# Second MoE of a three-layer kernel: row lists fetched by GpSimd through an index per partition, the late table in nine pieces, one-block row buffers and a third output buffer

## The chip, the cores and the metric

One core of one Trainium2 chip. The metric is the device time of one execution in microseconds. The kernel before takes 966.37 us (median of 3 runs, 966.15 to 967.48).

## The reference

Three layers follow one another: attention over 4 batches, 8 heads, 576 positions and 64 dimensions, with a threshold under the row maximum; a squared-ReLU feed-forward layer (512 to 2048 to 512) over the 2304 tokens, the first MoE; and a second MoE in which each token goes to one of eight experts:

```python
logits = x @ w_gate                       # 2304 x 8
e_idx = np.argmax(logits, axis=1)
...
gate_w = probs[np.arange(N), e_idx]
eom = 1.0 / (1.0 + np.exp(-(x @ w_output_gate)))
for e in range(E):
    mask = e_idx == e
    h = np.maximum(x[mask] @ w1[e], 0.0)  # w1[e]: 512 x 1024
    ye = h @ w2[e]                        # w2[e]: 1024 x 512
    out[mask] = gate_w[mask, None] * eom[mask, e, None] * ye
```

## The kernel before

**Planner.** The program is written as a graph of tasks (`Graph.add`), each with an engine, an estimated duration, what it reads and writes, and a due time, its `key`. `Graph.schedule` goes through them greedily: on each engine, of the tasks that could start within a small slack of the earliest, the one with the smallest key. Buffers come from pools (`mk` for on-chip memory, `mkps` for the product banks); a pool's slot may lie over another's that has to be done before. What comes out is one fixed order per engine. Each engine then works through its own queue in that order and stands where the head of the queue waits.

**First MoE's last tiles and the gate.** The 2304 tokens are 18 blocks of 128, two to a tile. For a tile v, `t_y` forms the layer's output from seven products (L1011) whose sums VectorE adds (L1021, L1027) into `row`; `t_gate` transposes the two blocks (L1161 on TensorE, L1166 ScalarE, L1167 VectorE), multiplies them by the gate's weights (L1076, transposed back at L1085), picks the expert (L1095 to L1107), ranks tokens by products with triangular matrices (L1113), computes each token's place in its expert's list (L1127 to L1133) and the gate's factor (L1138 to L1141). The rows with their factor go to DRAM (`y_scr`, L1151, SyncE's queue), and GpSimd scatters pairs (row, token) to their places in a DRAM list `lst` (L1147). The last tile, v = 8 (blocks 16 and 17), is called y8 below.

**Slots.** The second MoE runs in slots, each one expert's rows: "p" has 256 rows (two blocks), "s" 128, "W" 288 (two blocks and a remainder of 32). Two early slots, e0 and e1, use lists that an early table draws up when some tiles are done; they run while the first MoE ends. A late table (`t_table(False)`, L1206 to L1256 on VectorE, one task) sets up the rest: `tab2` for p, `tab1` for s, `tabw` for W, each with a list start and an expert number. The ten late slots follow the string `ORDER`. A branch on `tabn` (L1533, L1534), taken only if more slots are needed, stands within the last one.

`t_slot` does, for each slot: SyncE reads the list's start (`r_s`) and the expert (`r_e`) into registers; SyncE loads the slot's piece of `lst` (`f_list`, L1285; L1287 for a remainder); GpSimd gathers the rows of `y_scr` block by block into one three-block buffer `xg` (L1295); SyncE loads eight halves of a megabyte of weights into staging buffers `raw` (L1309 for w1, L1312 for w2; four buffers and a fifth); ScalarE and VectorE turn each into a rounded value and a remainder (L1316, L1319) in a pool `w`; the rows are transposed like those of the gate (L1161, L1166, L1167), and ScalarE copies each row's factor into `cs` (L1325, L1330). The first product (L1342, in 96 matmuls of 256 columns for a p slot; s has its own, L1363 with transposes L1375 behind ScalarE's L1369) leaves relu on ScalarE (L1350) and the remainder on VectorE (L1353). The second product is L1429 (48 of 512 columns) for p and s, evicted by L1438 into one of two buffers `ob` and scattered to the output by GpSimd (L1441); for W it is L1395, transposed back (L1409), evicted by L1414 and scattered by L1418. The output scatters wait for one another, since all write the one output.

## Time and profile before

| | before |
|---|---|
| time, median of 3 runs | 966.37 us (966.15 to 967.48) |
| profiled execution: time, span | 964.99 us, 963.2 us |
| mean granted TensorE clock | 0.987 |
| busy: TensorE, VectorE, ScalarE, GpSimd | 926.0, 706.8, 634.3, 360.7 us |
| span from e0's first product (687.90 us) to the end | 275.3 us |

The profile is of one execution. A row of its timeline gives the start, the duration, the engine and line, and in brackets how long the engine stood idle before it and what released it. Matmuls overlap, so a row of several lasts a little longer than their pitch. The granted clock is 1.00 at TensorE's upper level. Everything before 687 us is the attention and the first MoE and is the same program in both kernels but for the order of a few tasks.

### The profile page before, as it was taken

Reading aid. Unit: us, or ns where it says so; the run is one execution under the profiler, and the core shown is the slowest. Engines: PE = TensorE matmul, PEld = TensorE weight load, DVE = VectorE, ACT = ScalarE, POOL = GpSimd, SP = SyncE. Lnnn points to the kernel's source line nnn. Section 1 sums busy time; section 2 is a strip of 40 time slices with the busy share of each in tenths; the row PEclk is TensorE's granted clock in tenths of the full one; section 3 lists DMA queues with packets and bytes.
Section 4 is the critical chain, followed back from the end, with each engine's and each line's share of the span. In section 5 each row is a group of like instructions: output and inputs, shape, how many; then the busy total and the mean of one; then the engine's idle time right before and its main releaser. Section 6 shows DMA issues by size and latency. Waiting matters only on the chain.

```text
span 963.2 us, 20472 instructions
## 1 busy us (share of the span) xinstructions
PE 926.0 (96%) x6818; PEld 843.4 (88%) x6818; DVE 706.8 (73%) x1634; ACT 634.3 (66%) x1416; POOL 360.7 (37%) x607
## 2 busy tenths in 40 slices
PE   8889999999999999999999999999898999999995
PEld 7666889889899889889999999999887989889894
DVE  6888898877777777788558776898796685774720
ACT  5788888887787777686654544445546675775821
POOL 4556778766657767652100000010112221121200
PEclk9999999999999999999999999999898999999999
DMA  6785787767787767467456898648848895795700
GB/s 177 180 198 153 207 232 205 219 163 213 222 235 224 226 199 233 146 206 238 159 148 132 184 187 182 133 127 197 264 118 302 272 309 163 250 327 191 254 33 26
DMA packets 160534, 188.68 MB, mean 196 GB/s; under 512 B 23167, under 2 KB 112767, under 8 KB 160418
## 3 DMA queue, kind: packets, MB, share of 16 engines
q1 hardware_dynamic: 156370, 177.13, 65.4%
q0 software_dynamic: 3904, 10.13, 3.1%
q8 instruction: 57, 0.93, 0.4%
q14 instruction: 59, 0.48, 0.2%
q10 hardware_dynamic: 144, 0.00, 0.0%
HBM read 117.80 MB, written 42.80 MB: 167 GB/s over the span
## 4 chain that ended last, share of the span: by engine, by line
PE 69%; DMA 10%; DVE 7%; issue 6%; ACT 4%; POOL 2%; SPq 0%; POOLq 0%; DVEq 0%; ACTq 0%
PE banks L850 18%; PE banks L1011 17%; PE banks L1342 7%; PE banks L740 6%; PE banks L643 6%; PE banks L712 6%; PE banks L1429 5%; DMA memf<-y_scr,memf 3%; PE banks L1395 2%; DMA memf<-in_moe_w_dram 2%; ACT pt L720 1%; DMA out_dram<-memf 1%; PE banks L1161 1%; DVE memf L658 1%; PE banks L1363 1%
## 5 line engine op out<-in xcount | busy, mean ns | idle before, releaser
L658 DVE SCALAR_TENSOR_TENSOR memf<-banks,memf 128x576 f32<-128x576 f32 x144 | 116.3, 814 | 44.3 <-ACT memf L649 28.3
L850 PE MATMUL banks<-memr,w 128*128 128x288 f32 x960 | 145.0, 299 | 1.4 <-DVE memr L747 1.4
L850 PEld LDWEIGHTS banks<-memr,w 128*128 128x128 f32 x960 | 130.9, 188 | 5.4 <-issue 3.8
L1011 PE MATMUL banks<-w,memr 128*128 128x256 f32 x864 | 127.2, 285 | 0.0
L720 ACT ACTIVATE pt<-banks 128x384 f32<-128x384 f32 (+2 forms) x320 | 114.4, 419 | 14.7 <-PE banks L712 13.9
L646 DVE TENSOR_REDUCE memf<-banks 128x1 f32<-128x576 f32 x144 | 107.6, 750 | 18.0 <-PE banks L643 16.4
L649 ACT ACTIVATE memf<-banks,memf 128x576 f32<-128x576 f32 x144 | 107.1, 753 | 19.9 <-DVE memf L646 14.5
L991 ACT ACTIVATE memr<-memf 128x512 fp32r<-128x512 f32 x126 | 77.5, 630 | 61.5 <-PE banks L1011 51.4
L669 POOL TENSOR_SCALAR memf<-memf 128x576 f32<-128x576 f32 x136 | 112.5, 829 | 12.7 <-DVE memf L666 6.8
L643 PE MATMUL banks<-memr 128*128 128x288 f32 x592 | 110.0, 311 | 4.8 <-DVE memf L658 3.0
L712 PE MATMUL banks<-ident,memf 128*128 128x128 f32 x720 | 106.9, 278 | 5.9 <-ACT pt L720 5.1
L1011 PEld LDWEIGHTS banks<-w,memr 128*128 128x128 f32 x864 | 112.3, 190 | 0.3
L1011 PE MATMUL banks<-memr 128*128 128x256 f32 x648 | 98.7, 283 | 0.0
L712 PEld LDWEIGHTS banks<-ident,memf 128*128 128x128 f32 x720 | 85.6, 142 | 14.6 <-POOL memf L654 4.9
L887 POOL TENSOR_TENSOR memf<-memf 128x288 f32<-128x288 f32 x88 | 72.2, 829 | 65.5 <-DVE memf L887 41.9
L643 PEld LDWEIGHTS banks<-memr 128*128 128x128 f32 x592 | 84.7, 190 | 12.8 <-DVE memf L658 6.8
L1147 POOL DMA_INDIRECT lst<-memf x18 | 18.5, 1026 | 193.5 <-DVE memf L1139 115.9
L1319 DVE TENSOR_TENSOR w<-memf,w 128x512 fp32r<-128x512 f32 x110 | 72.6, 688 | 24.5 <-ACT w L1316 20.6
L995 DVE TENSOR_TENSOR memr<-memf,memr 128x512 fp32r<-128x512 f32 x126 | 83.0, 697 | 9.5 <-ACT memr L991 9.2
L850 PE MATMUL banks<-memr 128*128 128x288 f32 x576 | 87.9, 299 | 0.8 <-ACT memf L856 0.8
L1011 PEld LDWEIGHTS banks<-memr 128*128 128x128 f32 x648 | 86.7, 191 | 0.1
L740 PE MATMUL banks<-pt,memf 128*64 128x256 f32 (+1 forms) x640 | 85.1, 411 | 1.3 <-DVE memf L658 1.0
(181 smaller groups left out, 1761.2 us busy)
## 6 DMA issues: line engine op xcount, KB each, us to landing
memf<-in_moe_w_dram SPq DMA_DIRECT2D x96, 512.0 KB
r_scr<-memf SPq DMA_DIRECT2D x192, 144.0 KB
memf<-r_scr SPq DMA_DIRECT2D x51, 512.0 KB
memr<-memr SPq DMA_DIRECT2D x64, 144.0 KB
memr<-memr SPq DMA_DIRECT2D x64, 128.0 KB
memr<-memr SPq DMA_DIRECT2D x32, 256.0 KB
memf<-in_moe_w_in_dram SPq DMA_DIRECT2D x32, 256.0 KB
memf<-in_moe_w_out_dram SPq DMA_DIRECT2D x32, 256.0 KB
```

What stands on the lines that cost most here:

```text
L643: nc.tensor.matmul(s.t[:, hf, :HALF], qo, ko[:, halves[hf]], start=(i == 0), stop=(i == len(ops) - 1))
L646: nc.vector.tensor_reduce(nm.t, s.t[:, :, :HALF], axis=AX.XY, op=ALU.max, negate=True)
L649: nc.scalar.activation(p.t[:, :S].rearrange("p (a n) -> p a n", a=2), s.t[:, :, :HALF], AF.Exp, bias=nm.t)
L658: nc.vector.scalar_tensor_tensor(p3, s.t[:, :, :HALF], th.t, p3, op0=ALU.is_ge, op1=ALU.mult, accum_out=sm.t)
L669: nc.gpsimd.tensor_scalar(p.t[:, :S], p.t[:, :S], sm.t, 1.0, op0=ALU.mult, op1=ALU.mult)
L712: nc.tensor.transpose(ps.t[:, i - a], p.t[:, i * P : (i + 1) * P], ident)
L720: lambda pt=pt, ps=ps, j=j, a=a, z=z, c0=c0, w=w, off=off: nc.scalar.activation(pt.t[:, j, a:z, off : off + w], ps.t[:, :, c0 : c0 + w], A ...
L740: nc.tensor.matmul(out(slice(64 * j, 64 * j + 64)), raw.t[:, j, c], pt.t[:, j, c, :N], start=(c == 0), stop=(c == NQ - 1))
L850: nc.tensor.matmul(ps.t[:, :HALF], wv[:, a, kc], xT.t[:, x, kc, half], start=(i == 0), stop=(i == len(seq) - 1),)
L991: g.add("ACT", c_act(512), lambda d=d, sq=sq: nc.scalar.activation(d(0), sq(), AF.Copy), [(b, j)], [(o, 0, j)], at, after=turn["op"])
L995: lambda d=d, sq=sq: nc.vector.tensor_tensor(d(1), sq(), d(0).bitcast(F32), op=ALU.subtract),
L1011: nc.tensor.matmul(ps.t[:, :QT], o.t[:, a, f], w.t[:, x, cc], start=(f == 0 and i == 0), stop=(f == 7 and i == 2))
```

## The change

- Lists. `r_s` and `f_list` are gone from SyncE. GpSimd gathers each list by an index per partition: the constants `st2`, `st1` now hold the partition's number, so that a table's entry is the row of `lst` that this partition wants. For a slot of two blocks one indirect transfer fetches two pairs per partition; an s slot has one, a W slot three, through a new table `tabv`. These are 16 transfers more on GpSimd in the slots that run, and edges (`turn["lt"]`, `turn["xg"]`) keep lists and gathers in the slots' order.
- Late table. Its operations are collected and run in nine pieces, tasks of their own, with `tab2` done after the fourth piece (`tabl` stands for the rest); the early table stays in one piece.
- Buffers. Row buffers `xg`: three of one block in place of one of three. `ob`: three in place of two. `lt`, `cs`: four in place of three. `cs` is copied block by block. With the new sizes the fifth `raw` lies over other buffers of the first MoE (parts of p1, u2, u3, u4 and lgs instead of row1, gs, p1, u2 and u3).
- Due times. The last tile's sums and gate are due `HASTE` = 10 earlier; the early slots' transposes 3 earlier, and e1's come after the last gate's transposes (an `after` edge). `ORDER` is "psWspspsWp" instead of "psWspsWspp".

```diff
-    ORDER = "psWspsWspp"
+    HASTE = 10
+    ORDER = "psWspspsWp"
...
-    at = mk("lt", at, 3, [P, 3, 2], I32, 2)
-    at = mk("cs", at, 3, [P, 3], F32, 2)
+    at = mk("lt", at, 4, [P, 3, 2], I32, 2)
+    at = mk("cs", at, 4, [P, 3], F32, 2)
...
-    mk("xg", at, 1, [P, 3, DM + 1], F32, 3)
+    mk("xg", at, 3, [P, 1, DM + 1], F32, 3)
...
-    at = mk("ob", 0, 2, [P, DM], F32, 3)
+    at = mk("ob", 0, 3, [P, DM], F32, 3)
...
+        soon = lambda i: at(i) - (HASTE if v == TILES // 2 - 1 else 0)
...
-                out(4, 1, 0, "u3", at(i + 1))
+                out(4, 1, 0, "u3", soon(i + 1))
...
+        x = grp("PE", 0.45, tp, rd, [ps], key, hold=[x2], after=after)
...
+        for u in range(2):
+            ts(tabv[:, :, u], tabw[:, :, 0], 128.0 * (u + 1), None, op0=ALU.add)
...
-        grp("DVE", (3.1 if early else 8.4), run, [(c2, "base"), (c2, "tab")], [tb, "tabe" if early else "tabl"], key)
+            second(tt, ts, stt, copy, cnt, d, a, od, tmp, Q, wn, inc, cum, slots)
+
+        def piece(lo, hi):
+            if not prog:
+                run()
+                assert len(prog) == cuts[-1], (early, len(prog))
+            for x in prog[lo:hi]:
+                x()
+
+        cuts = [0, 19] if early else [0, 8, 15, 21, 27, 33, 39, 44, 50, 55]
+        for lo, hi in zip(cuts, cuts[1:]):
+            w = ["tabe" if early else "tab2" if hi <= 27 else "tabl"]
+            k = key if hi <= 27 else key + 10
+            grp("DVE", 0.195 * (hi - lo), lambda lo=lo, hi=hi: piece(lo, hi), [(c2, "base"), (c2, "tab")], [tb] + w, k)
...
-        td = "tabe" if tab is tabe else "tabl"
-        add("SP", 0.9, r_s, [td], [("reg", tag, 0)], key - 24)
-        dma(f_list, 2048, [("reg", tag, 0)] + deps, [lt], key - 24)
+        td = "tabe" if tab is tabe else "tab2" if tab is tab2 else "tabl"
+        if U == 2 and not R:
+            lists = [(range(2), lambda: lt.t[:, :2].rearrange("p u t -> p (u t)"), lst.rearrange("(r u) t -> r (u t)", u=2), tab[:, s, 0:1])]
+        else:
+            lists = [((u,), lambda u=u: lt.t[: rows(u), u], lst, (tabv[: rows(u), s, u - 1 : u] if u else tab[:, s, 0:1]))
+                     for u in range(UR)]
+        for us, dst, src, idx in lists:
+            add("POOL", 1.05,
+                lambda dst=dst, src=src, idx=idx: nc.gpsimd.indirect_dma_start(
+                    out=dst(), out_offset=None, in_=src, in_offset=bass.IndirectOffsetOnAxis(idx.bitcast(U32), 0)),
+                [td] + deps, [(lt, u) for u in us], key - 24, lat=3.0,
+                after=turn["lt"] if G is g else ())
...
-                [lt, "y0"] + [("ys", u) for u in range((rows_known - 1) // P)], [(xg, u)], key - 12, lat=6.5)
+                [(lt, u), "y0"] + [("ys", x) for x in range((rows_known - 1) // P)], [xg[u]], key - 12, lat=9.5,
+                after=turn["xg"] if G is g else ())
...
-            t_transpose(xg, u, x2, f"x{tag}", key - 8, [(xg, u)], G, pool, rows(u))
+            t_transpose(xg[u], u, x2, f"x{tag}", key - (11 if tab is tabe else 8), [xg[u]], G, pool, rows(u),
+                        turn["gate"] if tab is tabe and s == KE - 1 else ())
```

Three places in the orders. The first is VectorE near 690 us, where y8's last sums (L1021; L1026 in the changed kernel) stand among e0's weight remainders (L1319; L1355), each row's tile `w_..` or `memr` being a weight buffer; L1167 (L1173) is the remainder of transposed rows. Before:

```order
L1319 TENSOR_TENSOR w_71<-memf,w_71 128x512
L1319 TENSOR_TENSOR memr<-memf,memr 128x512
L1021 TENSOR_TENSOR memf<-banks,memf 128x256
L1319 TENSOR_TENSOR w_75<-memf,w_75 128x512
L1319 TENSOR_TENSOR w_78<-memf,w_78 128x512
L1167 TENSOR_TENSOR memr<-banks,memr 128x4x128
L1319 TENSOR_TENSOR memr<-memf,memr 128x512 x2
L1021 TENSOR_TENSOR memf<-banks,memf 128x256
```

After:

```order
L1173 TENSOR_TENSOR memr<-banks,memr 128x4x128
L1032 TENSOR_TENSOR memf<-banks,memf 128x256
L1026 TENSOR_TENSOR memf<-banks,memf 128x256
L1355 TENSOR_TENSOR w_71<-memf,w_71 128x512
L1355 TENSOR_TENSOR memr<-memf,memr 128x512
L1026 TENSOR_TENSOR memf<-banks,memf 128x256
L1355 TENSOR_TENSOR w_75<-memf,w_75 128x512
```

The last sum now stands behind the remainders of `w_71`, ahead of two pairs that it stood behind.

The second is VectorE at the late table: the end of the last tile's place (L1133) and the table's first rows in the kernel before, and a stretch of the table (all its rows bear the line L1204) in the changed one, with L1353 (L1387), e0's relu remainder, and L1319 (L1355). Before:

```order
L1132 TENSOR_REDUCE memf<-memf 128x2
L1133 CAST memf<-memf 128x2
L1353 SCALAR_TENSOR_TENSOR memr<-banks,memr 128x256
L1206 TENSOR_TENSOR memf<-memf 128x8
L1207 COPY memf<-memf 128x8
```

After:

```order
L1204 TENSOR_TENSOR memf<-memf 128x64
L1204 TENSOR_REDUCE memf<-memf 128x8
L1204 TENSOR_TENSOR memf<-memf 128x8
L1204 CAST tabn<-memf 128x1
L1204 TENSOR_TENSOR memf<-memf 128x8
L1204 SCALAR_TENSOR_TENSOR memf<-memf 128x8
L1355 TENSOR_TENSOR memr<-memf,memr 128x512
L1204 TENSOR_TENSOR memf<-memf 128x96 x3
L1204 TENSOR_TENSOR memf<-memf 128x192
L1204 TENSOR_REDUCE memf<-memf 128x24
L1204 TENSOR_TENSOR tab_91<-memf 128x24
L1387 SCALAR_TENSOR_TENSOR memr<-banks,memr 128x256
```

The table's rows ran on to L1256 without another line between; now relu and weight remainders stand between the pieces. `tab_91` is `tab2`.

The third is GpSimd's queue from e1's gathers to p0's: list scatters L1147 (L1153), row gathers L1295 (L1328), list gathers (L1319, new), output scatters L1441 (L1475). Before:

```order
L1147 DMA lst<-memf 21760x2 x4
L1295 DMA memf<-y_scr,memf 128x513 x2
L1147 DMA lst<-memf 21760x2 x2
L1441 DMA out_dram<-memf 2304x512 x2
L1295 DMA memf<-y_scr,memf 128x513 x2
L1441 DMA out_dram<-memf 2304x512
L1295 DMA memf<-y_scr,memf 128x513
L1441 DMA out_dram<-memf 2304x512
```

After:

```order
L1328 DMA memf<-y_scr,memf 128x513
L1153 DMA lst<-memf 21760x2 x4
L1328 DMA memf<-y_scr,memf 128x513
L1153 DMA lst<-memf 21760x2 x2
L1319 DMA memf<-lst,tab_91 128x4
L1475 DMA out_dram<-memf 2304x512
L1328 DMA memf<-y_scr,memf 128x513 x2
L1475 DMA out_dram<-memf 2304x512
L1319 DMA memf<-lst,tab_92 128x2
L1319 DMA memf<-lst,tabw 128x2
```

The list gather of p0 (`tab_91`) stands right behind the last list scatters; of the two output scatters of e0 that stood before p0's row gathers, one now stands before them and one behind.

## Rows read from the trace of the kernel before

**Rows 1.** The page, part 1: busy time of each engine.

```profile
PE 926.0 (96%) x6818; PEld 843.4 (88%) x6818; DVE 706.8 (73%) x1634; ACT 634.3 (66%) x1416; POOL 360.7 (37%) x607
```

**Rows 2.** Windows by stage: start:end, length, busy time per engine (instructions), granted clock, DMA.

```profile
687.90:720.04 32.14, 28.68 (x171) 25.33 (x170) 27.23 (x104) 15.64 (x35) 1.98 (x2) 0.89 0.53 171
720.04:751.49 31.45, 26.92 (x154) 23.40 (x152) 22.75 (x41) 19.84 (x40) 8.60 (x6) 0.89 0.85 297
751.49:829.50 78.01, 76.66 (x491) 69.33 (x490) 53.08 (x91) 55.58 (x113) 14.31 (x13) 1.00 0.74 246
```

**Rows 3.** Waits of TensorE, 640 to 964 us: total, times, longest.

```profile
PE banks L1161 <- DMA memf<-y_scr,memf: 4.3, 3, 3.7
PE banks L1161 <- DVE memf L1021: 2.8, 1, 2.8
PE banks L1375 <- ACT memf L1369: 2.6, 2, 1.3
PE banks L1429 <- PEq L1534: 1.8, 1, 1.8
```

**Rows 4.** Timeline of TensorE: start, duration, operation, [idle before <-releaser].

```profile
693.14 1.11 PE L1161 MATMUL banks<-ident,memf 128*128 128x128 f32 x4 [2.78 <-DVE memf L1021]
...
694.48 0.41 PE L1342 MATMUL banks<-memr 128*128 128x256 f32 x1
...
700.15 0.28 PE L1342 MATMUL banks<-memr,w 128*128 128x256 f32 x1
...
721.56 5.01 PE L1342 MATMUL banks<-memr,w 128*128 128x256 f32 x40 [0.41 <-DVE memr L1167]
...
740.20 1.12 PE L1161 MATMUL banks<-ident,memf 128*128 128x128 f32 x4 [3.74 <-DMA memf<-y_scr,memf]
...
742.48 2.91 PE L1429 MATMUL banks<-memr 128*128 128x512 f32 x6
...
762.69 1.55 PE L1429 MATMUL banks<-memr 128*128 128x512 f32 x6
```

**Rows 5.** Timeline of VectorE, 700 to 724 us.

```profile
701.90 0.19 DVE L1095 COPY memf<-banks 128x32 f32<-128x32 f32 x1
...
706.73 0.17 DVE L1133 CAST memf<-memf 128x2 uint32<-128x2 f32 x1
...
707.14 0.16 DVE L1206 TENSOR_TENSOR memf<-memf 128x8 f32<-128x8 f32 x1
...
712.28 0.18 DVE L1203 TENSOR_TENSOR tab<-memf 128x24 int32<-128x24 f32 x1
...
717.07 0.16 DVE L1256 SCALAR_TENSOR_TENSOR tabn<-tabn,memf 128x1 int32<-128x1 int32 x1
...
721.42 2.49 DVE L1319 TENSOR_TENSOR w<-memf,w 128x512 fp32r<-128x512 f32 x4
```

**Rows 6.** Timeline of ScalarE.

```profile
690.79 1.15 ACT L1316 ACTIVATE memr<-memf 128x512 fp32r<-128x512 f32 x2 [0.32 <-DMA memf<-in_moe_w_dram]
...
822.27 0.68 ACT L1414 ACTIVATE memf<-banks,memf 32x512 f32<-32x512 f32 x1 [1.72 <-DMA out_dram<-memf]
```

**Rows 7.** Timeline of SyncE's queue, 715 to 722 us.

```profile
715.84 3.08 SPq L1312 DMA_DIRECT2D memf<-in_moe_w_dram  x2
...
721.57 0.38 SPq L1285 DMA_DIRECT2D memf<-lst  x1
```

**Rows 8.** Timeline of GpSimd, 712 to 734 us, and landings of `y_scr` transfers.

```profile
712.92 0.98 POOL L1147 DMA_INDIRECT lst<-memf  x1 [4.75 <-DMA lst<-memf]
721.71 3.08 POOL L1441 DMA_INDIRECT out_dram<-memf  x1 [7.81 <-ACT memf L1438]
731.03 0.99 POOL L1441 DMA_INDIRECT out_dram<-memf  x1 [6.24 <-DMA memf<-in_moe_w_dram]
732.32 0.98 POOL L1295 DMA_INDIRECT memf<-y_scr,memf  x1 [0.30 <-PE banks L1342]
...
DMA to landing us min/median/max: 3.6/5.8/8.1
```

More of the change, by code (lines that the diff above doesn't have):

```diff
@@ L249, in tables @@
     ctab[:, lo : lo + n] = np.arange(128)[:, None] < np.arange(128)[None, :]
+    for nm in ("st2", "st1"):
+        lo, n = CTAB[nm]
+        ctab[:, lo : lo + n : 2] += np.arange(128)[:, None]
     p = np.arange(512)
@@ L502, in moa @@
     tabw = const.tile([P, NLW, 2], I32, name="tabw")
+    tabv = const.tile([P, NLW, 2], I32, name="tabv")
     tabn = const.tile([P, 4], I32, name="tabn")
@@ L916, in moa @@
         at += n
-    assert at <= 528, at
+    assert at <= 536, at
     def cv(nm, shape=None, dt=F32):
@@ L963, in moa @@
     rows = {}
-    turn = {"op": [], "slot": 0}
+    turn = {"op": [], "slot": 0, "xg": [], "lt": []}
     def t_y(v, key):
@@ L1055, in t_gate @@
         for i in range(2):
-            t_transpose(row, i, x2, f"y{v}", key + i - 1, [(row, i, 0), (row, i, 1)])
+            turn["gate"] = [t_transpose(row, i, x2, f"y{v}", key + i - 1, [(row, i, 0), (row, i, 1)])]
         lt = Buf(ALL["lgt"], f"lgt{v}")
@@ L1168, in t_transpose, with second, later @@
             [ps, (x2, 0, i)], [(x2, 1, i)], key)
+        return x
     tb = Buf(ALL["tb"], "tb")
-    def t_table(early, key):
-        tt, ts, stt = nc.vector.tensor_tensor, nc.vector.tensor_scalar, nc.vector.scalar_tensor_tensor
+    def second(tt, ts, stt, copy, cnt, d, a, od, tmp, Q, wn, inc, cum, slots):
+        tt(cnt, d, a, op=ALU.add)
+        cum(od)
+        copy(tabn[:, 1:2], inc[:, 7:8])
+        stt(Q[:, 0], cnt, 256.0, ct("ebd"), op0=ALU.mult, op1=ALU.add)
+        slots(NL1, tab1, False)
+        cum(wn)
+        copy(tabn[:, 2:3], inc[:, 7:8])
+        stt(Q[:, 0], od, 128.0, Q[:, 0], op0=ALU.mult, op1=ALU.add)
+        slots(NLW, tabw, False)
+        for u in range(2):
+            ts(tabv[:, :, u], tabw[:, :, 0], 128.0 * (u + 1), None, op0=ALU.add)
+        ts(tmp[:, 0:1], tabn[:, 0:1], float(S2), None, op0=ALU.subtract)
+        stt(tmp[:, 0:1], tabn[:, 1:2], float(S1), tmp[:, 0:1], op0=ALU.subtract, op1=ALU.max)
+        stt(tabn[:, 3:4], tabn[:, 2:3], float(SW), tmp[:, 0:1], op0=ALU.subtract, op1=ALU.max)
+    def t_table(early, key):
+        prog = []
+        def later(fn):
+            return lambda *a, **k: prog.append(lambda: fn(*a, **k))
+        tt, ts, stt = (later(x) for x in (nc.vector.tensor_tensor, nc.vector.tensor_scalar, nc.vector.scalar_tensor_tensor))
+        copy, reduce = later(nc.vector.tensor_copy), later(nc.vector.tensor_reduce)
         def run():
@@ L1273, in t_slot @@
         turn["slot"] += 1
-        lt, xg, cs, x2, hT = (Buf(pool[x], f"{x}{tag}") for x in ("lt", "xg", "cs", "x" + side, "h" + side))
+        lt, cs, x2, hT = (Buf(pool[x], f"{x}{tag}") for x in ("lt", "cs", "x" + side, "h" + side))
+        xg = [Buf(pool["xg"], f"xg{tag}_{u}") for u in range(U + (R > 0))]
         regs = {}
@@ L1489, in moa @@
             K3 = K2 + TILES // 2 * TY
-            for s in range(KE):
-                t_slot(g, ALL, f"e{s}", tabe, s, 2, 1 + TE * P, ["lst"] + [("lst", x) for x in range(TE)], K3 + s * 22)
+    for s in range(KE):
+        t_slot(g, ALL, f"e{s}", tabe, s, 2, 1 + TE * P, ["lst"] + [("lst", x) for x in range(TE)], K3 + s * 22)
     t_table(False, K3 + 2)
```

95 lines of the change are left out of this document (38 added, 57 removed).

## The prediction

> **What bounds the kernel now.** I read the page's first part, then the busy time by stage, then TensorE's waits, then the rows around each wait. TensorE is busy 926.0 of 963.2 us [rows 1], so little can come from anywhere but its gaps. The stage table [rows 2] shows where they lie: the first early slot of the second MoE (e0) has 28.68 of 32.14 us busy at a granted clock of 0.89, the second (e1) 26.92 of 31.45 at 0.89, while the next 78 us run at 1.00 and are busy but for 1.35. TensorE's waits from 640 us on [rows 3] are few: 4.3 for gathered rows, 2.8 for VectorE's L1021, 2.6 for ScalarE's L1369, 1.8 for its own sequencer at the branch L1534. The change leaves that last one alone.
>
> The first two cost more than they last. After the 2.78 us at 693.14 one L1342 takes 0.41 us where it takes 0.28 at 700.15; after the 3.74 us at 740.20 six L1429 take 2.91 where they take 1.55 at 762.69 [rows 4]. [...] The waits of 1.3 us in rows 3 had no such tail.
>
> **What each wait hangs on.** At 693.14 TensorE transposes the last row block of the first MoE (y8). Its sum, L1021, was what came last [rows 4]: VectorE had it queued, by the order, behind weight remainders (L1319) whose weights ScalarE got at 690.79 [rows 6]. The 3.74 us are the rows of p0, the first late slot. Their chain starts with the gate's place at 706.73 [rows 5]. SyncE's queue stands before the fifth staging load L1312 until 715.84, when the second scatter of the list, issued at 712.92, has landed, 2.9 us later, and reaches the list load L1285 only at 721.57 [rows 7]. GpSimd then stands 6.24 us before the second L1441, and issues the gather L1295 at 732.32 [rows 8]. That is 33 us from place to rows.
>
> **Part by part.** Durations are those of the profiled execution, 964.99 us (span 963.2 and 1.79 around it); the median shown is 1.38 above it.
>
> 1. *e0's stage (HASTE, gate ahead, e1's transposes behind the gate).* Its work at the full clock is 96 L1342 at 0.119 to 0.121 (40 take 5.01), 48 L1429 at 0.232 (six take 1.55, the first 0.39; both [rows 4]) and 1.9 of transposes and gate, about 24.4 us; 32.14 − 24.4 = 7.7 are lost. By the order, y8's second block is now transposed after 12 L1342 instead of after 12 and e1's block, and the last L1021 stands two pairs of conversions earlier on VectorE. I put the block's sum at 690.0, which leaves TensorE some 0.9 us; the gate product L1076 waits 0.7 to 1.2 for the remainder conversion behind two weight pairs, L1085 up to 1.0. Taken: 2.4 lost, gaps too short for a slow tail. Bounds: 0, and 5.9, as now (2.98 idle and 2.9 of clock). **Gain 5.3.**
>
> 2. *The late table.* 53 small VectorE operations run in one block from L1206 at 707.14 to L1256 at 717.07 [rows 5], 10 us, with L1353 held behind them. The nine pieces do the same and two operations more for tabv (10.3 us), with conversions between. They cost no less VectorE time. Count from t0, the start of the expert's pick (701.90 now [rows 5], about 695 after, since the gate comes earlier): pick, gate and place 3.7 (4.99 from 701.90 to 706.89 [rows 5], less two L1353 and one L1319 between), table 10.3, 16 conversions and 2 remainders at 0.60 (four take 2.49 [rows 5]), 6 L1353 at 0.34: 26.8 before e1's first L1353. TensorE needs it at t0+26.0, when its fifth group of products wants a bank. So **about 1.2 us of wait remains in e1's first product**, hidden until now by the later start.
>
> 3. *List gathers on GpSimd, and what they free on SyncE.* Twelve slots lose a value load and their list loads on SyncE, and GpSimd issues 16 more indirect transfers, each about 0.98 us of its queue like L1147 [rows 8]. GpSimd has 14.31 us of work in the 78 us after p0's rows [rows 2], so issue itself is hidden. What counts is p0's chain: place ends at t0+4.7; first scatter 0.3 later; second 5.75 later (712.92, 4.75 idle and 0.99 of issue [rows 8]); landed 2.9 later [rows 7]; list gather 1.0 and 2.9 to 5.75; row gather 5.8 (median) to 8.1 [rows 8]. Rows lie at t0+22.9 to t0+28.0. TensorE wants them at t0+25.7 with its e1 work moved up. Late table and rows wait in parallel, so I take **1.5 us lost in e1's stage** for both, bounds 0 and 10 with 2.9 of clock. Now e1 loses 31.45 − 23.0 = 8.4 (23.0 by the same pitches). **Gain 6.9.** tab2 is ready after piece four, of ten microseconds now at 712.28 [rows 5], so the table isn't what p0 waits for. The fifth raw buffer's new place also takes away its wait until 715.84, so one e1 weight is asked for some 8 us earlier; that is cover for 1 and 2.
>
> 4. *Three output buffers.* The third L1414 stood until 822.27, [1.72 <-DMA out_dram] [rows 6], and L1369 behind it made TensorE wait; twice, 2.6 in all [rows 3]. With a third buffer each of the three blocks has its own. **Gain 2.6**; bounds 0 (a scatter still in flight from the slot before) and 2.6.
>
> 5. *Row buffers one block each, four lists, scales copied per block.* The last ScalarE copy L1325 held all of a three-block buffer; now a gather waits for its own block alone. Extra: one copy of 0.2 us per block. Nothing taken: rows of later slots are already there in time (rows 3 show none). The cover is GpSimd's lead over TensorE; if it is gone, rival F follows.
>
> Sum: 964.99 − 5.3 − 6.9 − 2.6 = 950.2; with the 1.38 to the median, **951.6 us**.
>
> [...] One L1441 took 3.08 us to issue instead of 0.98 [rows 8], and just then VectorE ran four L1319 in 2.49 us without a gap [rows 5]. [...]
>
> **The rivals.**
> - *B, weights still set e0's pace.* L1021 and the gate stay behind conversions whose weights land no earlier: loss 5.9 instead of 2.4. For: the waits before L1316 in rows 6 end on landings. Against: the last L1021 moves ahead of the two pairs that held it. 951.6 + 3.5 = **955.1**.
> - *C, GpSimd slow beside VectorE.* If the two scatters, the list and the row gather each take 3.08 instead of 1.0, p0's rows come at t0+28.0+8.4 = t0+36.4, 10.7 late, with 2.9 of clock: 13.6 instead of 1.5. **963.7**. For: the row of 3.08, as VectorE is fuller with table pieces among conversions. Against: the other rows of group 8, all 0.98 or 0.99.
> - *D, all hidden*: neither e0's nor e1's stage loses. **947.7**.
> - *E, the change does not do what it says*: p0's chain stays 33 us long because another link (the out scatters ahead of the row gathers) takes its place, and e0 gains nothing net: **966**.
> - *F, slower.* At p2 GpSimd's queue holds, by the order, the three scatters of W0, the list, s1's scatter, then p2's rows; each scatter waits for the one before to land (6.24 [rows 8]). 2.9 + three of 6.4 + list 7.5 (1.0 and a landing as slow as a scatter's) + rows 9.4 (1.3 and the 8.1 of [rows 8]) = 39 us, and TensorE reaches p2's transposes 39.5 after (by the order and the pitches 13.3 of s1, 22.6 of p1, 3.5 of the next). It fits by half a microsecond; three more microseconds on each of five links make 14.6 late, with 2.9 of clock: **969**. For it speaks that lists were on SyncE, out of this queue; against it that nothing in that stretch has shown a landing over 8.1.
>
> **How the numbers follow.** Forecast 0.45, B 0.22, C 0.15, D 0.10, E 0.03, F 0.05. From D's 947.7, less 0.7 for execution and rounding, to below C's upper end the range 947 to 961 holds forecast, B, D and the milder half of C: about 0.84 of it. A measurement of this kernel tells about 0.2%, 1.9 us, from no change. All but E and F lie below 964.4: faster 0.92, same 0.03, slower 0.05.
>
> **What would show it.** In the stage table e0 should take about 27 us and e1 about 24.5, both at a clock of 0.97 or more; TensorE's wait on L1369 should be gone; the wait for row gathers at p0 under 2 us; a wait on L1353's successor near 1 us at e1's start should be new. The prediction is wrong if p0's rows still arrive later than 30 us after pick, if a list gather lands after more than 6 us, if e0's stage still shows a clock of 0.89, or if a new wait appears at p2 or W1.

## The result, and the profile after

The changed kernel takes 956.48 us (median of 4 runs, 951.37 to 958.76), the kernel before on the same occasion 966.26 (4 runs, 962.29 to 967.48): a ratio of 0.9896, 95% interval 0.9859 to 0.9934. Run again on another occasion it took 957.88 (10 runs) against 964.54 (17 runs), 0.993 (0.9904 to 0.9956). So it is faster by 7 to 10 us, about 1%, inside the range of 947 to 961, and 5 to 6 us above the forecast of 951.6. Ten or more runs of either kernel on one chip spread over 9 to 14 us, and the median of the kernel before lay between 959.3 and 966.3 us on four occasions. Stages are therefore compared by profiles, and by several of them.

The profiled execution took 958.76 us, span 956.6, mean granted clock 0.993. Its stages, in the columns of [rows 2]; e0 from 690.07, e1 from 720.70, p0 from 745.40:

```profile
690.07:720.70 30.63, 27.40 (x170) 23.98 (x169) 27.07 (x96) 17.31 (x39) 4.10 (x4) 0.94 0.75 203
720.70:745.40 24.70, 23.53 (x153) 21.25 (x152) 22.69 (x52) 18.47 (x39) 12.15 (x11) 1.00 0.95 315
745.40:823.00 77.60, 77.60 (x502) 70.66 (x501) 54.76 (x94) 56.61 (x117) 15.33 (x14) 1.00 0.77 265
```

e1 went from 31.45 to 24.70 us at a clock of 1.00, e0 only from 32.14 to 30.63. Between the two profiles the span fell by 6.5 us: 1.5 were gained in e0, 6.75 in e1 and 1.7 in the late slots (203.6 to 202.0), while 2.2 were lost ahead of e0, whose first product came at 690.07 instead of 687.90, and 1.25 behind the last product. Busy VectorE (the third pair, 27.07 of 30.63 and 22.69 of 24.70) is worth noting now. TensorE's waits, which answer to [rows 3]:

```profile
PE banks L1463 <- PEq L1568: 1.9, 1, 1.9
PE banks L1082 <- ACT memr L1172: 1.3, 1, 1.3
PE banks L1167 <- DVE memf L1026: 1.3, 1, 1.3
PE banks L1167 <- DMA memf<-y_scr,memf: 1.2, 1, 1.2
PE banks L1082 <- DVE memr L1173: 0.6, 1, 0.6
```

The wait for L1369 (here L1403) behind the W slots is gone and the gathered rows cost 1.2 instead of 4.3. New are waits at the gate product L1082 (before, L1076), for ScalarE and VectorE. Its rows, with what followed them:

```profile
692.94 0.66 PE L1167 MATMUL banks<-ident,memf 128*128 128x128 f32 x4 [1.30 <-DVE memf L1026]
...
696.30 0.30 PE L1082 MATMUL banks<-memr 128*32 128x256 f32 x1 [1.31 <-ACT memr L1172]
697.23 1.56 PE L1082 MATMUL banks<-memr 128*32 128x256 f32 x7 [0.62 <-DVE memr L1173]
698.59 1.05 PE L1167 MATMUL banks<-ident,memf 128*128 128x128 f32 x4
```

Three waits of 1.30, 1.31 and 0.62 us lie within five microseconds; seven L1082 then take 1.56 us and four transposes 1.05 where they take 0.60 to 0.66 elsewhere: the granted clock was 0.59 from 697.20 to 698.50 and 0.50 from 698.60 to 700.00, after gaps that I had called too short for that. ScalarE shows what L1082 waited for, the copy L1172 of the last block at 695.68:

```profile
693.31 1.16 ACT L1352 ACTIVATE w<-memf 128x512 fp32r<-128x512 f32 x2 [2.49 <-DMA memf<-in_moe_w_dram]
694.62 1.15 ACT L1352 ACTIVATE memr<-memf 128x512 fp32r<-128x512 f32 x2 [0.15 <-DMA memf<-in_moe_w_dram]
695.68 0.58 ACT L1172 ACTIVATE memr<-banks 128x512 fp32r<-128x512 f32 x1
```

It stood behind two weight pairs that landed only at 693.3 and 694.6, though TensorE had transposed the block at 692.94. That is rival B. The chain to p0's rows, on GpSimd, which answers to [rows 8]:

```profile
705.17 0.98 POOL L1153 DMA_INDIRECT lst<-memf  x1 [18.50 <-DVE memf L1139]
710.31 0.96 POOL L1153 DMA_INDIRECT lst<-memf  x1 [4.16 <-DMA lst<-memf]
717.09 1.09 POOL L1319 DMA_INDIRECT memf<-lst,tab  x1 [5.82 <-DVE w L1355]
718.48 1.07 POOL L1475 DMA_INDIRECT out_dram<-memf  x1 [0.30 <-issue]
723.12 0.98 POOL L1328 DMA_INDIRECT memf<-y_scr,memf  x1 [3.56 <-PE banks L1376]
```

Counted from the pick at 700.03: second scatter 10.3, list gather 17.1, row gather 23.1, rows at TensorE 27.65 (the row below), inside the 22.9 to 28.0 of the prediction and 10.7 earlier than the 38.3 before.

```profile
727.68 0.55 PE L1167 MATMUL banks<-ident,memf 128*128 128x128 f32 x3 [1.17 <-DMA memf<-y_scr,memf]
```

### The profile page after: what moved, and what is told of

It is laid out like the page before. It is cut to its first block, busy times and chain, and to the rows that moved or that the text cites. A ratio compares the mean times of both kernels' runs of the same rounds, so it can differ in the third digit from the quotient of the medians.

```text
span 956.6 us, 20411 instructions
## 1 busy us (share of the span) xinstructions
PE 924.1 (97%) x6818; PEld 842.6 (88%) x6818; DVE 707.0 (74%) x1636; ACT 635.1 (66%) x1424; POOL 374.7 (39%) x623
## 4 chain that ended last, share of the span: by engine, by line
PE 77%; DMA 8%; DVE 5%; issue 4%; ACT 3%; POOL 2%; SPq 0%; POOLq 0%; DVEq 0%; ACTq 0%
PE banks L855 18%; PE banks L1016 18%; PE banks L1463 8%; PE banks L1376 7%; PE banks L745 6%; PE banks L648 6%; PE banks L717 6%; DMA out_dram<-memf 4%; PE banks L1397 2%; PE banks L1167 2%; DVE memf L663 2%; PE banks L1429 1%; DVE memf L651 1%; ACT memf L654 1%; ACT pt L725 1%
## 5 line engine op out<-in xcount | busy, mean ns | idle before, releaser
L663 DVE SCALAR_TENSOR_TENSOR memf<-banks,memf 128x576 f32<-128x576 f32 x144 | 116.2, 814 | 44.7 <-ACT memf L654 27.7
L1016 PE MATMUL banks<-w,memr 128*128 128x256 f32 x864 | 126.7, 284 | 0.0
L651 DVE TENSOR_REDUCE memf<-banks 128x1 f32<-128x576 f32 x144 | 107.5, 750 | 17.4 <-PE banks L648 14.7
L648 PE MATMUL banks<-memr 128*128 128x288 f32 x592 | 110.1, 311 | 6.3 <-DVE memf L663 4.0
L1016 PEld LDWEIGHTS banks<-w,memr 128*128 128x128 f32 x864 | 112.0, 190 | 0.3
L1016 PE MATMUL banks<-memr 128*128 128x256 f32 x648 | 98.2, 282 | 0.0
L648 PEld LDWEIGHTS banks<-memr 128*128 128x128 f32 x592 | 84.6, 190 | 15.0 <-DVE memf L663 7.8
L717 PEld LDWEIGHTS banks<-ident,memf 128*128 128x128 f32 x720 | 84.6, 141 | 13.9 <-POOL memf L659 3.9
L1153 POOL DMA_INDIRECT lst<-memf x18 | 18.7, 1041 | 181.7 <-DVE memf L1145 109.3
L1016 PEld LDWEIGHTS banks<-memr 128*128 128x128 f32 x648 | 86.3, 190 | 0.1
L1355 DVE TENSOR_TENSOR w<-memf,w 128x512 fp32r<-128x512 f32 x110 | 72.8, 688 | 15.8 <-ACT w L1352 14.8
```

The costliest lines, as they stand in the source:

```text
L648: nc.tensor.matmul(s.t[:, hf, :HALF], qo, ko[:, halves[hf]], start=(i == 0), stop=(i == len(ops) - 1))
L651: nc.vector.tensor_reduce(nm.t, s.t[:, :, :HALF], axis=AX.XY, op=ALU.max, negate=True)
L663: nc.vector.scalar_tensor_tensor(p3, s.t[:, :, :HALF], th.t, p3, op0=ALU.is_ge, op1=ALU.mult, accum_out=sm.t)
L717: nc.tensor.transpose(ps.t[:, i - a], p.t[:, i * P : (i + 1) * P], ident)
L1016: nc.tensor.matmul(ps.t[:, :QT], o.t[:, a, f], w.t[:, x, cc], start=(f == 0 and i == 0), stop=(f == 7 and i == 2))
```

## The experiments

In all of them a stage's length is read from the profile as above: e0 from its first L1376 to e1's first, e1 to p0's first, the late slots from there to the last product, the end from there to the end of the span. The stretch ahead of e0, from the first L648 (L643 in the kernel before) to e0's first product, took 672.4 to 675.9 us in the fourteen profiles without regard to the edit, so a few us between two spans say little.

Medians are compared within a chip only. In us, with the number of runs:

| chip | kernel before | versions of the changed kernel |
|---|---|---|
| first | 964.54 (17) | unaltered 957.88 (10), gate ahead 955.02 (6), table in one piece 955.04 (4), `HASTE` 0 953.41 (6) |
| second | 961.86 (25) | two output buffers 951.77 (10), lists on SyncE 949.62 (4), later landings 955.18 (10) |
| third | 959.26 (17) | old order of the slots 949.46 (4), old staging place 949.94 (4), last five pieces later 948.45 (4), that and lists on SyncE 959.36 (12) |

The unaltered changed kernel is the slowest of its chip's four. It was not timed on the second and third, so no time shows how the versions there stand to it.

**The changed kernel and the kernel before, unaltered.**

> The changed kernel once more, unaltered. Theory (the profiled execution's 2.2 us of late start and the clock loss of 1.6 us behind the branch are its own, not the change's): e0's stage 30.6 us and e1's 24.7 again, each within 0.8, TensorE's waits at the last tile's gate (1.3, 1.3 and 0.6 us) there again; the start of the first L648 and the clock behind the branch may differ. Rival (those two losses belong to the change): first L648 again near 14.6 us, and 19 L1463 behind the branch again in 6.0 us.

Measured: 957.88 us; e0 29.16, e1 28.20 (3.3 us of it wait for p0's rows), waits at the last tile's sum and gate of 1.7, 0.5, 0.6 and 0.4 us. The start was late again (first L648 at 14.66), but the loss behind the branch was not there, by an estimate: with the pick 9.1 us after e0's start, the two stages, the span of 957.5 and an end of 9.24 to 9.38, the late slots took 200.4 to 200.5 us, against 202.0 in the first profile. Both stages missed the expectation, e0 by 1.4 us downwards and e1 by 3.5 upwards: p0's rows reached TensorE 29.2 us after the pick (728.67 after 699.46), behind the 28.0 of the prediction.

> The kernel before once more, unaltered, for a second profile of it. Theory (its stages vary little from execution to execution; the 2.2 us at the program's start and the 1.2 us behind the last product that the changed kernel's profiles show on top are not the change's doing at the start, but are at the end): e0's stage 32.1 and e1's 31.5 us, each within 1; the end, from the last product to the end of the span, again 8.1 us, where all profiles with the lists on GpSimd show 9.2 to 9.4; the first L643 anywhere from 12.4 to 14.7 us. Rival: the end is 9.3 here too, so that it is of the execution.

Measured: 960.02 us (8 runs) against 961.86 (25 runs) for the same kernel on that chip; e0 28.83, e1 27.13, the late slots 203.90, the end 8.04, the first L643 at 14.03. The end is as the theory has it, but both stages missed the expectation, and that matters most for the prediction:

```profile
688.30:717.13 28.83, 25.79 (x171) 22.61 (x170) 26.23 (x103) 14.64 (x34) 2.02 (x2) 1.00 0.54 180
717.13:744.26 27.13, 24.03 (x153) 21.26 (x152) 22.64 (x41) 19.76 (x40) 7.61 (x6) 1.00 0.92 330
```

```profile
PE banks L1161 <- DMA memf<-y_scr,memf: 2.7, 2, 2.1
PE banks L1161 <- DVE memf L1021: 2.4, 1, 2.4
```

The waits of [rows 3] are there again, somewhat shorter (2.4 where 2.78 was, 2.7 in all where 4.3 was, the longest 2.1 where 3.74 was), but the clock stayed at 1.00 behind both. So e0 and e1 together took 55.96 us in one execution of the kernel before and 63.57 in the other. The one that was read had lost more clock than nearly any other: its mean granted clock over the whole execution was 0.987, the second's 0.992, and of 67 timed executions of this kernel on three chips four were at 0.987 or below, with a median of 0.992.

**The gate ahead of the weights.** For the planner alone, e0's weights land later:

```diff
-            dma(fetch, 524288, [("reg", tag, 1)], [raw], kj - 12)
+            add("SP", 1.542, fetch, [("reg", tag, 1)], [raw], kj - 12, lat=c_dma(524288) - 1.542 + (6 if tab is tabe and s == 0 else 0))
```

> Only the planner's landing time for e0's weights is raised by 6 us, so that in ScalarE's queue the copy of the last tile's second block stands behind four weight pairs instead of seven and the gate comes ahead of the pairs that land last. Theory (e0 still loses 6 us because ScalarE and VectorE hold the gate's steps behind conversions of weights that land late): TensorE's waits at L1082 (1.9 us) go, the clock stays up, e0's stage falls from 30.6 to 27.0 (26.3 to 28.0) and the time by about 3. Rival (the weights themselves set e0's pace, the gate only shows it): the wait moves to e0's products L1376 or L1463, behind L1355, and the stage stays above 29.5.

Measured: 955.02 us (6 runs); e0 27.03, TensorE's waits at L1082 gone, clock 1.00. The theory holds for the waits. In e0 there are new ones of 0.4 and 1.1 us for L1387, VectorE's relu remainder. e1 took 26.75, with 0.9 us of wait for L1387 and 1.8 for p0's rows.

```profile
690.68:717.71 27.03, 25.52 (x167) 22.05 (x165) 23.04 (x80) 16.59 (x37) 3.26 (x3) 1.00 0.85 210
717.71:744.46 26.75, 24.03 (x154) 21.32 (x153) 25.62 (x65) 18.95 (x39) 15.46 (x11) 1.00 0.86 290
```

The length of e0 flatters this version, though. The last block's transposes and the wait for its sum stand here ahead of e0's first product, outside the stage, while they lie inside it in the changed kernel:

```profile
688.16 1.59 PE L1016 MATMUL banks<-w,memr 128*128 128x256 f32 x12
690.26 0.66 PE L1167 MATMUL banks<-ident,memf 128*128 128x128 f32 x4 [0.52 <-DVE memf L1026]
690.68 0.36 PE L1376 MATMUL banks<-memr 128*128 128x256 f32 x1
```

From the end of the last L1016, the first MoE's last product, to e1's first product it took 28.0 us here and 27.9 in the three later versions with this edit. The changed kernel took 30.5 and 29.0, and two more profiles with its orders in e0 and e1 (two output buffers and the old order of the slots, below) 29.1 and 27.6. So the gate ahead avoids the long cases, but is no shorter than the good one; in time the runs of the two kernels overlap (952.95 to 959.68 here, 952.49 to 961.59).

**The table in one piece.**

```diff
-        cuts = [0, 19] if early else [0, 8, 15, 21, 27, 33, 39, 44, 50, 55]
+        cuts = [0, 19] if early else [0, 55]
...
-            w = ["tabe" if early else "tab2" if hi <= 27 else "tabl"]
+            w = ["tabe"] if early else ["tab2", "tabl"]
```

> The late table in one piece again, all else as in the changed kernel. Theory (p0's list waits for the landing of the last list scatter, not for the table, so the pieces are worth little): p0's list gather is issued within 1 us of the same time after the place step as now (12.2 us), e1's stage stays at 24.7 within 0.7, and e0's stage grows by at most 0.7 for the L1387 that stands behind ten microseconds of table. Rival (the pieces carry the gain in e1): the table's block delays relu remainders and weight remainders so that e0 and e1 together take 3 us or more longer.

Measured: 955.04 us (4 runs); e0 27.79, e1 30.78 at a clock of 0.89. The theory's first number fell: the list gather came 24.94 us after the pick, 20.3 after the place, since with one late piece the planner put both of e0's output scatters ahead of it on GpSimd. e0 and e1 together took 58.6, against 52.0 to 57.4 in four profiles with the pieces and the changed kernel's orders. TensorE waited 2.8 us for p0's rows and 1.2 for L1387, so in this profile the loss comes by way of GpSimd's order more than of VectorE's time. But it was the slowest of four executions (959.55 us, the others 953.42 to 956.02), and their median lies 2.8 us below the changed kernel's on that chip: that the pieces are worth anything in time is not shown.

**The due times.** `HASTE = 0`.

> HASTE 0 in place of 10, all else as in the changed kernel: the last tile's sums and gate are due when they were before. Theory (the earlier due times are what e0 has gained, and the gate's time sets the late slots' lists): the second block's transposes wait again 2 us or more, e0's stage is 32 us or more, and the pick comes 2 us or more later. Rival (e0 is held by its weights whatever the due times): e0's stage within 0.7 of 30.6.

Measured: 953.41 us (6 runs), e0 29.04, e1 24.98 with no wait for p0's rows; the pick came 11.2 us after e0's start, against 10.0 and 9.1 in the changed kernel and 7.7 in the two other profiles with its orders. The theory falls, and the rival's number was missed too, by 0.9 us downwards. e0 lies within the 27.7 to 30.6 of the four profiles with the earlier due times, and the time is 4.5 us below the changed kernel's on the same chip (950.56 to 957.70 against 952.49 to 961.59): the earlier due times gave nothing that can be told. Without them p0's transposes stood together, later, in TensorE's order, and no longer caught the rows' lateness.

**Two output buffers**, their neighbours' addresses kept:

```diff
-    at = mk("ob", 0, 3, [P, DM], F32, 3)
+    at = mk("ob", 0, 2, [P, DM], F32, 3) + 512
```

> Two output buffers in place of three, their neighbours left where they are; the orders of TensorE, GpSimd and SyncE are those of the changed kernel. Theory (the third buffer frees ScalarE at the W slots): TensorE's waits for L1402, the relu of the s slot behind W, come back, 1.3 us at each of two places, 2.6 in all, from p0's start to the last product. Rival (the new order of the slots, or landings, have changed what stands behind W): below 0.8 us in all.

Measured: 951.77 us (10 runs); late slots 202.1, and one wait, behind W0, for the s slot's relu (its line is L1403; the text above names the one before it):

```profile
810.75 0.66 PE L1409 MATMUL banks<-ident,memf 128*128 128x128 f32 x4 [1.57 <-ACT memf L1403]
```

With three buffers and the same slots they take 200.3 to 200.6 in three profiles where the clock holds behind the branch (in one of them, with later landings, six L1463 take 1.55 us there, against 2.31 in the changed kernel's first profile at a clock of 0.62 to 0.65), and 201.1 with the last five pieces later. So the third buffer is worth the wait of 1.6 us here; behind W1 there is no s slot in the new order that could wait. e0 and e1, whose orders on TensorE, GpSimd and SyncE are those of the changed kernel, took 53.0 together, e0 at a clock of 0.94 again: these orders have shown 53.0, 55.3 and 57.4, and 52.0 in the next run.

**The old order of the slots**, `ORDER = "psWspsWspp"`:

> The old order of the slots, psWspsWspp, in the changed kernel. Before, from p0's start to the last product took 203.6 and 203.9 us; in the changed kernel it takes 200.3 to 200.5 where TensorE's clock holds behind the branch, 202.1 with two output buffers. Theory (the third buffer is half of these 3.4 us and the new order of the slots the other half): 201.9 to 202.3 with the clock held, no wait of TensorE for L1402. Rival (the order is worth nothing, one-block row buffers or lists give the rest): 200.2 to 200.8.

Measured: 949.46 us (4 runs); late slots 200.4, no wait for L1403. The rival holds: with three buffers the order is worth nothing, and either of the two removes the wait at the second W slot. Before, the late slots took 203.6 and 203.9. In e0 and e1 every engine has the changed kernel's order, and the two took 52.0, with waits at the last tile's sum and gate of 0.5, 0.6 and 0.7 us:

```profile
687.07:714.79 27.72, 25.90 (x171) 22.74 (x169) 25.56 (x92) 16.35 (x37) 4.13 (x4) 1.00 0.76 217
714.79:739.03 24.24, 23.65 (x153) 21.28 (x152) 22.60 (x54) 17.80 (x38) 12.42 (x10) 1.00 0.91 312
```

**The fifth staging buffer in its old place:**

```diff
-    at = mk("ob", 0, 3, [P, DM], F32, 3)
-    at = mk("h32", at, 2, [P, 512], F32, 3)
-    at = mk("raw", at, 1, [P, 2, 512], F32, 3)
+    at = mk("ob", 0, 3, [P, DM], F32, 3)
+    mk("raw", 2048, 1, [P, 2, 512], F32, 3)
+    mk("h32", at, 1, [P, 512], F32, 3)
+    at = mk("h32", 3072, 1, [P, 512], F32, 3)
```

> The fifth staging buffer back where it lay before the change (over the gate's scratch and others), its neighbours moved around it; all else as in the changed kernel. Theory (its new place is what lets e1's weights come early, and so what gives e1 its gain): SyncE stands before the next weight load until the last list scatter has landed, 16 to 19 us after the pick, e1's stage is 28 us or more with a wait for weight remainders or conversions. Rival (e1 is held by VectorE and by p0's rows, not by weights): e0 and e1 together 54 to 58 us, as in the changed kernel's two profiles (55.3 and 57.4).

Measured: 949.94 us (4 runs); e0 27.91, e1 24.93, together 52.8. SyncE did stand until 708.34, 13.9 us after the pick, and TensorE waited 1.0 us for a weight remainder, but e1 is no longer than in the changed kernel. The theory falls; the rival's 54 to 58 was missed too, downwards. This holds with the lists on GpSimd; with both the lists and the buffer as before it was not run.

**The lists on SyncE again**, tables and constants as before the change:

```diff
+        def f_list():
+            nc.sync.dma_start(lt.t[:, :U], lst[bass.ds(regs["s"], U * P)].rearrange("(u p) t -> p u t", p=P))
...
+        add("SP", 0.9, r_s, [td], [("reg", tag, 0)], key - 24)
+        dma(f_list, 2048, [("reg", tag, 0)] + deps, [(lt, u) for u in range(UR)], key - 24)
```

> The lists on SyncE again (register loads and plain transfers, tables and constants as before the change), everything else as in the changed kernel. Theory (p0's rows wait on two list scatters, one after the other, and on landings, whoever issues the list): SyncE reaches p0's list some 1 to 4 us later than GpSimd did, p0's first rows come 28 to 33 us after the pick instead of 27.7 to 30, e1's stage is 25 to 30 us. Rival (the lists on GpSimd are what carries e1's gain): the list waits in SyncE's queue behind weights until 35 us after the pick, rows 38 us after it as before, e1's stage 31 us or more.

Measured: 949.62 us (4 runs), 0.9884 of the kernel before (0.9812 to 0.9956); e0 27.85, e1 24.74, together 52.6; p0's row gather 21.6 us after the pick, earlier than in the changed kernel's two profiles (23.1 and 24.0), no wait for rows. Both theories missed: SyncE's list was not later at all. SyncE loaded it at 711.90, 16.4 us after the pick, where it came 19.7 after it in the kernel before ([rows 7]). So moving the lists to GpSimd is not what gained e1. GpSimd's order differs as well: in [rows 8] both output scatters of e0 stand ahead of p0's row gathers, here one of them stands behind:

```profile
711.24 1.39 POOL L1471 DMA_INDIRECT out_dram<-memf  x1 [4.12 <-ACT memf L1468]
717.06 1.02 POOL L1324 DMA_INDIRECT memf<-y_scr,memf  x1 [4.42 <-DMA memf<-lst]
718.39 0.97 POOL L1324 DMA_INDIRECT memf<-y_scr,memf  x1 [0.30 <-issue]
719.66 1.02 POOL L1471 DMA_INDIRECT out_dram<-memf  x1 [0.30 <-issue]
```

In the three profiles with both scatters ahead (the two of the kernel before and the table in one piece) the first row gather went out 30.0 to 32.1 us after the pick, in the other eleven 19.6 to 25.6. No run moves that scatter alone, so that it carries e1's gain is likely, not shown. And the end is shorter:

```profile
939.67 1.54 PE L1459 MATMUL banks<-memr 128*128 128x512 f32 x6
```

```profile
span 949.2 us, 20491 instructions
```

From 941.21, the end of the last product, 8.0 us are left. The changed kernel's last product ended at 945.82 + 1.54 = 947.36, with 9.24 left. All four profiles with the lists on SyncE (the two of the kernel before, this one and the last one of this section) show 7.99 to 8.09, the other ten 9.24 to 9.38.

**Later landings for the list too.** As the first of these edits, with the last tile's list scatters landing after 8 us and p0's list after 6 for the planner:

```diff
-                [(gs, 2), (c2, "coln"), "lst"], [("lst", u)], key, lat=2.5)
+                [(gs, 2), (c2, "coln"), "lst"], [("lst", u)], key, lat=8 if v == TILES // 2 - 1 else 2.5)
...
-                [td] + deps, [(lt, u) for u in us], key - 24, lat=3.0,
+                [td] + deps, [(lt, u) for u in us], key - 24, lat=6.0 if tab is tab2 and s == 0 else 3.0,
```

> Only the planner's landing times are raised: e0's weights by 6 us, the last tile's list scatters to 8, p0's list to 6. In the order the gate stands ahead of the last weight pairs, and p0's two transposes stand together behind e1's first 18 products of the second kind. Theory (the two losses left are queue orders planned with landings that are too early): e0's stage 27.0 (26.3 to 28.0), no wait for p0's rows, e1's stage 24 to 26 with 1 to 2.5 us of wait for L1387 (VectorE is full with the table's pieces); the time 2 to 5 us below the unaltered changed kernel's 957.9. Rival (what one stage gives, the next takes: the rows or weights come no sooner): e0 and e1 together 55 us or more, as in the changed kernel (55.3 and 57.4).

Measured: 955.18 us (10 runs); e0 26.95, no wait for rows, but e1 28.30, together 55.25. The rival holds: what e0 gave, e1 took, through VectorE. On the same chip the version with two output buffers, which lacks all of these edits, took 951.77 us (10 runs, 948.88 to 954.75, against 951.32 to 959.12 here): by this the later landings alone make the kernel slower, not faster. The pick, e1's first L1387 on VectorE and TensorE's wait for it:

```profile
691.47 0.19 DVE L1101 COPY memf<-banks 128x32 f32<-128x32 f32 x1
```

```profile
722.64 1.41 DVE L1387 SCALAR_TENSOR_TENSOR memr<-banks,memr 128x256 fp32r<-128x256 f32 x4
```

```profile
723.11 0.39 PE L1376 MATMUL banks<-memr 128*128 128x256 f32 x1 [3.22 <-DVE memr L1387]
```

The remainder came 31.2 us after the pick, behind the table's last five pieces and weight remainders; the 3.22 us were followed by a lower clock (0.94 over e1).

**The last five pieces later**, added to the kernel just shown:

```diff
-            k = key if hi <= 27 else key + 10
+            k = key if hi <= 27 else key + 30
```

> The kernel with the raised landing times once more, and the table's last five pieces due 20 later, so that VectorE does e1's first three relu remainders (L1387) ahead of four of them. Theory (with the gate early, VectorE is what bounds e1: its first L1387 stood behind five pieces and four weight remainders, 31.2 us after the pick, and cost 3.2 us of wait and a stretch at the lower clock): the wait for L1387 falls from 4.7 to below 1.5 us, e1's stage from 28.3 to 24.0 to 25.5, e0 and e1 together to 51 to 52.5. Rival (VectorE's work is only put off: 49 us of it lie in these two stages whatever the order): the wait comes back later in e1 or at p0's transposes, e0 and e1 together 54 us or more.

Measured: 948.45 us (4 runs, 947.09 to 948.77) against 959.26 (17 runs) on that chip, 0.988 (0.9837 to 0.9923). Its stages and waits:

```profile
685.83:712.76 26.93, 25.47 (x167) 22.26 (x166) 23.52 (x79) 16.58 (x37) 4.75 (x4) 1.00 0.81 213
712.76:736.10 23.34, 23.34 (x153) 21.25 (x152) 22.58 (x62) 17.16 (x36) 9.36 (x8) 1.00 0.86 295
```

```profile
PE banks L1376 <- DVE memr L1387: 1.5, 2, 1.1
```

The theory holds for the waits and for e1: 23.34 us, with TensorE busy throughout; the 1.5 us of wait for VectorE that are left lie in e0. This version beats the kernel before. e0 and e1 together took 50.3, but e0 again lacks what stands ahead of its first product: from the end of the last L1016 to p0's first product it took 51.2 us, the run with the old order of the slots 51.8; from the same mark to the last product of all they took 252.3 and 252.2. On the same chip that run took 949.46 us and the one with the old staging place 949.94, within 1.5 us of this version: that it is faster than the changed kernel is not shown.

**Both: lists on SyncE and the later pieces.** The edits of the last two together with the lists on SyncE.

> What seems best of all: lists on SyncE again, raised landing times, the table's last five pieces later, the rest (three output buffers, one-block row buffers, order of the slots, place of the fifth staging buffer) as in the changed kernel. Theory: e0 and e1 together 51 to 52.5 us, the end 8.0 us, p0's start to the last product 200.3 to 200.8: a span of 946 to 948 where the start is an early one, a median near 947 to 949, 3 to 5 us below the version with the lists on SyncE alone is not excluded. Rival (run to run differences at the start and in the clock cover it): no better than that version's 949.6.

Measured: 959.36 us (12 runs), 1.0008 of the kernel before (0.9983 to 1.0033): a miss of 11 us. e0 and e1 took 50.25, the end 8.01, as expected. But the late slots took 209.6. W0's list, its rows and TensorE's wait:

```profile
767.20 0.39 SPq L1315 DMA_DIRECT2D memf<-lst  x1
```

```profile
769.80 1.19 POOL L1324 DMA_INDIRECT memf<-y_scr,memf  x1 [6.42 <-PE banks L1459]
```

```profile
777.08 1.12 PE L1164 MATMUL banks<-ident,memf 128*128 128x128 f32 x4 [4.32 <-DMA memf<-y_scr,memf]
779.07 1.11 PE L1164 MATMUL banks<-ident,memf 128*128 128x128 f32 x4 [0.88 <-DMA memf<-y_scr,memf]
```

The list load of W0 stood in SyncE's queue behind weight loads until 767.20, the rows came 4.32 us late, and the products behind that ran slower: two L1372 took 0.68 us from 781.54 on and 0.43 from 785.66. With the lists on SyncE alone this load stood at 751.59, 11.2 us after p0's first product instead of 29.6, and with the lists on GpSimd and the same later pieces TensorE waited for no rows here either. So it takes both the later pieces and SyncE's queue, and this is the only place in these runs where a list on GpSimd paid.

## Why the prediction was right, point by point, and where it was not

**The direction and the two places were right.** The gain lies in e0, e1 and behind the W slots, GpSimd kept up at p2 (no wait for rows behind p0's; rival F did not occur), and its issues in p0's chain took 0.96 to 1.09 us, not 3 (rival C's mechanism did not occur there; single issues of 2.1 to 3.7 us are in seven of the fourteen profiles, one of them a list gather of 3.03 us in the run with the table in one piece). The trace shows p0's list gather issued in 1.09 us while VectorE was 27.07 of 30.63 us busy in e0.

**e0: the step that failed is "2.4 lost, gaps too short for a slow tail".** 6.2 us were lost of 30.63, at a clock of 0.94 where 0.97 or more was said. L1026 and the transposes behind it came at 692.9, 1.3 us late where 0.9 was said; the gate product then waited 1.31 and 0.62 behind weight pairs landing at 693.3 and 694.6, and behind the three gaps the clock fell to 0.50. Rival B, 5.9, is what happened in that execution, and the run with the gate ahead shows the cause of the waits: there they are gone. The three other profiles with the same orders lost 4.8, 4.8 and 3.3 us, the 3.3 at a clock of 1.00, so the forecast was too low in all four, but part of the 6.2 is of the execution. The work of 24.4 us was too low as well: the second profile of the kernel before has TensorE busy for 25.79 us of e0 at a clock of 1.00.

**e1: the gain came out, its cause and two links of the chain did not.** 6.75 us were gained for 6.9 said, but the forecast put them down to the lists on GpSimd and what they free on SyncE, and with the lists back on SyncE e1 took 24.74. That the number fits is in part luck. The 2.9 us from second scatter to landing were the release of SyncE in [rows 7], which I took for the landing; the list gather in fact went out 6.7 to 6.8 us after the scatter (717.09 after 710.31). The row gather made up for it with 4.6 instead of 5.8 to 8.1. TensorE waited 1.17 us for the rows in one profile and 3.35 in the next, for 1.5 said. The links as listed add up to 23.4 to 28.5, not 22.9 to 28.0. One of the signs of being wrong did come: a list gather landed after 6.1 us in the first profile and after 8.9 in the second, for 6 at most, but TensorE waited for no rows except p0's.

**VectorE's bill was right, and did not fall due.** The forecast put e1's first relu remainder 26.8 us after the pick; it came after 26.9 (726.92). The wait of 1.2 did not show, since e0 ended late; at e1's start it did in other versions (0.9 with the gate ahead, 1.4 with `HASTE` 0, 3.2 with the later landings).

**Three output buffers: 2.6 said**, of 3.3 that the late slots gained; the run with the old order shows that the new order adds nothing to the rest of the change, the one with two buffers that the third is worth 1.6 under the new order. Two buffers in the old order, with the other edits, were not run; the waits that the two profiles of the kernel before show there are 2.6 and 2.9.

**The sum's main error is what it was made against.** Of the 12.2 us for e0 and e1, 5.8 were clock lost behind two waits, 2.9 behind either; the 2.9 of clock in the prediction's bounds and rivals is the same count. In that profile the granted clock was 0.50 from 693.10 to 697.00 and from 742.00 to 745.00. 24 L1342 stood 0.213 us apart instead of 0.119, and their four transposes took 1.11 instead of 0.60 to 0.66; behind the second wait eight transposes took 2.24 instead of 1.20 to 1.32, and 30 L1429 took 9.0 from 742.48 to 751.49 instead of 7.0 at 0.232 each. A second profile of the kernel before has somewhat shorter waits and no such loss, at a clock of 1.00. From 63.6 and 56.0 (mean 59.8) the stages went to 55.3, 57.4, 53.0 and 52.0 (mean 54.4): 5.4 us. With 3.3 from the late slots, less 1.2 at the end, that is 7.5, between the 6.7 and 9.8 of the medians; with two profiles before and a spread of 5 us after, it is no more than a rough agreement. The forecast also took 0.2%, 1.9 us, for the least change that can be told; the two intervals are 0.5% and 0.75% wide. That the 2.2 us of later start in the changed kernel's first profile are of the execution is shown by the others, where it lies at 12.5, 13.5 or 14.7 without regard to the edit, and in the kernel before at 12.45 and 14.03.

**Open:** what decides in an execution whether the clock falls behind a gap of 2 us (behind the branch it fell after 1.83 to 1.91 us in four profiles, in three of which six of the products that follow took 2.31 to 2.77 us, and held after 1.68 to 2.12 in the other ten, in six of which the same six took 1.53 to 1.55), why landings of the same small transfers differ by several us from run to run, and what of e1's gain is due to the one-block row buffers, the four lists and the row scales copied by block, which no run undoes by themselves.

## What to carry to other kernels

Take two or three profiles of the kernel before you price a stage: its waits come again, but the clock lost behind them may not, and here 5.8 of the 12.2 us expected from two stages were such a loss. When a wait goes, ask which queue was hidden behind it: the gate's ScalarE copy stood behind weights that land late, and behind that stood VectorE, busy for 50 of 55 us in the two stages. Measure a stage between marks that the edit does not move, and check its gain against the time on one chip: the gate ahead shortened e0 partly by moving work out of it, and landings nearer to the trace's, given to the planner, did not pay by themselves.

## What the runs showed that was not expected

- Lists on GpSimd lengthen the end of the program by 1.2 us: from the last product to the end of the span 9.24 to 9.38 in ten profiles with them, 7.99 to 8.09 in four without, with the same last scatter. No run tells where in the end these 1.2 us lie.
- An indirect transfer of 8 or 16 bytes for each of 128 partitions lands hardly sooner than one of 2 KB rows: list gathers 4.2 to 6.1 us (median 5.0) in the changed kernel's first profile and 2.9 to 8.9 (5.0) in its second, row gathers 3.3 to 9.1 (median 5.7) and 3.1 to 8.3 (5.1).
- One wait of 4.3 us in a late slot, at a place with no slack behind it, cost more than everything gained in e0 and e1: 209.6 against 200.8 us, of which 5.2 were idle.
